# One level of Strassen for h on 11 pairs of row tiles, with a new order of the work

## The chip, the core and the metric

The kernel runs on one core of a Trainium2 chip. The metric is the device time of one execution in microseconds (us). TensorE (PE) does the matrix products, VectorE (DVE), ScalarE (ACT) and GpSimd (POOL) the elementwise work, and SyncE (SP) issues the DMAs. Each engine works through its own queue in order; semaphores join the queues.

## The reference, cut to what matters

A linear attention over 8 batches of 8 heads (576 positions, 64 wide) gives x of 4608 rows by 512. Then comes the layer that the change is about:

```python
h = x @ w_in                                  # 4608x512 by 512x1024
e = np.exp(h - h.max(-1)); sm = e / (e.sum(-1) + 1e-9)
solu = h * sm
ln = (solu - mean) / sqrt(var + 1e-6) * g_ln  # over each row's 1024
out = ln @ w_out                              # 1024x512
```

## The kernel before

The 4608 rows are 36 row tiles of 128 rows, named by batch and part and numbered 0 to 35 in the order in which they are made. Batches with an odd number have a fifth tile, which holds the last 64 rows of two batches.

The work is cut into generators, one for each key, and `ORDER` is a list, written out by a planner, of which generator takes its next step. The list is the program order: what it places on one engine runs there in that order. A suffix `.v` puts a step that has a choice on VectorE in place of ScalarE or GpSimd; `*3` means three steps. The keys are: `LK`, `LQ`, `V` loads; `K3` the keys of batch 3 up to the head matrices `bd`; `Q3a`, `Q3c`, `R3` the query softmaxes; `w0` to `w3` and `y0` to `y3` the two weight matrices, which come as 64-bit words and are put together on ScalarE and VectorE; `W` and `Z` their scaling and their split in two f16 halves (a high half and what is left, `wi[:, 0]` and `wi[:, 1]`, likewise `wo`); `P` idle matmuls that fill TensorE early on.

For each row tile t, `x` (L613 to L625) makes the transposed x in PSUM and copies it to SBUF as `xT`, again as a high and a low f16 half; two tiles share one such step. `h` (`hidden`, L640 to L704) makes h in a PSUM tile of two banks, of which there are two (`bufs=2`): 12 terms (high by high, low by high, high by low, over four chunks of 128 rows of w_in) times two halves of 512 columns, 24 matmuls of 128x512. The first four tiles are done in f32 instead (L640). The row's tail then works on h in PSUM: the maximum `top` on VectorE (L655), `nm` and the exponential `e` on ScalarE (L657, L661), a scale `ph` in tiny steps on GpSimd (L665 to L674), `h*ph*e` on VectorE (L677), `nmu`, the f16 high half `u` on ScalarE (L679, L682), the low half on VectorE (L684), the square on ScalarE (L691). A PSUM tile is free for the next h after that square. `u` is transposed by DMA into `uT` (L687), and `o` (`project`, L722) makes the output from `uT` and `wo` in 24 matmuls, later in the list.

Of the kernel before, what the change touches and what calls it, by code (L numbers as in the profile page):

```python
# [843 lines left out]
```

## Time and profile before

| | us |
|---|---|
| median of three runs | 457.14 (457.02 to 457.19) |
| profiled execution, first to last instruction (span) | 455.4 |
| around the span, median less span | 1.7 |
| busy: TensorE | 435.4 |
| busy: VectorE | 337.5 |
| busy: ScalarE | 276.0 |
| busy: GpSimd | 209.2 |

Times are of the one profiled execution; busy means that an instruction of the engine runs. A group's mean is the mean length of one instruction; since a next one can begin before the one in front has ended, the means add up to more than the busy time.

### The profile page before, as it was taken

The numbers are of one execution on the slowest core, as the hardware profiler recorded it, in microseconds if no ns is written. First come the engines' busy times: TensorE is split into PE (matmuls) and PEld (weight loads), VectorE is DVE, ScalarE is ACT, GpSimd is POOL, SyncE is SP. The second block draws the span as 40 slices with busy tenths as digits, with TensorE's granted clock in tenths as the row PEclk, the third lists the DMA queues.
The fourth block names the chain that finished last, engine by engine and source line by source line (L and its number), as shares of the span: only waits on it lengthen the run. The fifth ranks groups of instructions, "written<-read, shape, count | busy, mean of one in ns | idle before, by whom it ended". The sixth has DMA issues, their size and how long they took to land.

```text
span 455.4 us, 8734 instructions
## 1 busy us (share of the span) xinstructions
PE 435.4 (96%) x3351; PEld 208.4 (46%) x3351; DVE 337.5 (74%) x619; ACT 276.0 (61%) x477; POOL 209.2 (46%) x334
## 2 busy tenths in 40 slices
PE   0898899999999999999999999999999999999996
PEld 0543344454445445444544445444454444444445
DVE  5999999989788898769967869777967565443410
ACT  3889998685866656466657566556657444441331
POOL 4107885886774355734363375712423234211120
PEclk9999999999999999999999999999999999999999
DMA  8997699699779994996884787884436425334071
GB/s 276 394 317 276 124 199 173 166 224 185 176 155 211 199 244 63 221 212 148 180 210 91 158 190 167 191 201 97 107 64 136 94 46 117 69 79 84 24 186 46
DMA packets 167082, 73.98 MB, mean 162 GB/s; under 512 B 146424, under 2 KB 155904, under 8 KB 167040
## 3 DMA queue, kind: packets, MB, share of 16 engines
q1 hardware_dynamic: 167040, 73.42, 68.7%
q8 instruction: 26, 0.43, 0.4%
q14 instruction: 16, 0.13, 0.1%
HBM read 36.70 MB, written 9.44 MB: 101 GB/s over the span
## 4 chain that ended last, share of the span: by engine, by line
PE 87%; DVE 5%; DMA 3%; ACT 3%; issue 1%; POOL 1%; ACTq 0%; DVEq 0%; POOLq 0%
PE o L722 41%; PE h L648 37%; PE x L613 4%; PE kv L425 4%; DMA w_out<-in_moe_w_out_dram 2%; DMA qm<-in_q_dram 1%; PE h L640 1%; DVE qnmx L475 1%; DVE h L677 1%; DVE iw L269 1%; PE warm_up L779 1%; DVE iw L267 0%; POOL am L665 0%; ACT qm L479 0%; ACT e L691 0%
## 5 line engine op out<-in xcount | busy, mean ns | idle before, releaser
L722 PE MATMUL o<-wo,uT 128*128 128x512 f16 (+1 forms) x888 | 198.3, 373 | 0.0
L648 PE MATMUL h<-wi,xT 128*128 128x512 f16 x768 | 177.1, 379 | 0.0
L722 PEld LDWEIGHTS <-uT 128*128 128x128 f16 x888 | 85.7, 98 | 98.0 <-issue 1.8
L648 PEld LDWEIGHTS <-xT 128*128 128x128 f16 x768 | 74.3, 98 | 89.4 <-issue 1.0
L655 DVE TENSOR_REDUCE top<-h 128x1 f32<-128x1024 f32 x36 | 43.9, 1218 | 27.6 <-PE h L648 27.4
L684 DVE SCALAR_TENSOR_TENSOR u<-h,nmu,u 128x1024 f16<-128x1024 f32 x36 | 46.0, 1277 | 15.6 <-ACT u L682 15.2
L691 ACT ACTIVATE e<-h,nmu 128x1024 f32<-128x1024 f32 x36 | 40.0, 1112 | 25.4 <-DVE u L684 25.2
L677 DVE SCALAR_TENSOR_TENSOR h<-h,ph,e 128x1024 f32<-128x1024 f32 x36 | 46.3, 1285 | 7.9 <-POOL ph L674 4.6
L665 POOL TENSOR_SCALAR am<-nm 128x1 f32<-128x1 f32 x25 | 10.3, 412 | 88.6 <-ACT nm L657 88.6
L671 POOL TENSOR_TENSOR p<-pi,mone 128x1 f32<-128x1 f32 x36 | 24.2, 671 | 55.1 <-DVE pi L668 53.5
L682 ACT ACTIVATE u<-h,nmu 128x1024 f16<-128x1024 f32 x36 | 40.1, 1113 | 1.0
L732 ACT ACTIVATE os<-o,rr 128x512 f32<-128x512 f32 (+1 forms) x23 | 15.5, 674 | 31.9 <-PE o L722 16.6
L657 ACT ACTIVATE nm<-top,hs 128x1 f32<-128x1 f32 x28 | 8.2, 294 | 43.4 <-DVE top L655 43.4
L661 ACT ACTIVATE e<-h,nm,hs 128x1024 f32<-128x1024 f32 x28 | 33.7, 1203 | 0.7
L679 ACT ACTIVATE nmu<-s 128x1 f32<-128x1 f32 x36 | 7.3, 202 | 42.0 <-DVE h L677 39.8
L640 PE MATMUL h<-iw,xT 128*128 128x512 f32 x64 | 29.8, 601 | 2.4 <-ACT e L691 2.3
L502 POOL TENSOR_TENSOR qhl<-qm,qhl 128x512 f16<-128x512 f32 x24 | 28.1, 1191 | 7.2 <-ACT qhl L162 4.6
L495 POOL TENSOR_TENSOR qm<-qm,qrec 128x1024 f32<-128x1024 f32 x12 | 23.6, 1969 | 11.7 <-DVE qrec L486 10.7
L625 DVE SCALAR_TENSOR_TENSOR xT<-x,xT 128x512 f16<-128x512 f32 (+1 forms) x36 | 22.2, 622 | 8.5 <-ACT xT L623 8.5
L477 POOL TENSOR_TENSOR qm<-qm,qnmx 128x1024 f32<-128x1024 f32 (+1 forms) x12 | 23.5, 1964 | 8.4 <-DVE qnmx L475 8.4
L730 DVE TENSOR_SCALAR os<-o,rr 128x512 f32<-128x512 f32 (+1 forms) x14 | 10.2, 728 | 20.4 <-PE o L722 20.4
L623 ACT ACTIVATE xT<-x 128x512 f16<-128x512 f32 (+1 forms) x36 | 19.2, 542 | 8.5 <-PE x L613 8.5
(155 smaller groups left out, 539.4 us busy)
## 6 DMA issues: line engine op xcount, KB each, us to landing
km<-in_k_dram SPq DMA_DIRECT2D x7, 1152.0 KB, 7.5
vm<-in_v_dram SPq DMA_DIRECT2D x28, 288.0 KB, 4.5
out_dram<-os SPq DMA_DIRECT2D x31, 256.0 KB, 3.2
qm<-in_q_dram SPq DMA_DIRECT2D x7, 1024.0 KB, 6.4
wo<-in_moe_w_in_dram SPq DMA_DIRECT2D x4, 512.0 KB, 8.6
w_in<-in_moe_w_in_dram SPq DMA_DIRECT2D x4, 512.0 KB, 9.4
wo<-in_moe_w_out_dram SPq DMA_DIRECT2D x4, 512.0 KB, 5.6
w_out<-in_moe_w_out_dram SPq DMA_DIRECT2D x4, 512.0 KB, 8.9
```

What stands on the lines that cost most here:

```text
L495: on(nc.gpsimd).tensor_tensor(x, x, wide(rec), op=ALU.mult)
L502: on(nc.gpsimd).tensor_tensor(lo, y, hi, op=ALU.subtract)
L640: nc.tensor.matmul(h[:, ns], xT[:, kc], iw[kc][:, ns], start=(i == 0), stop=(i == NP - 1))
L648: nc.tensor.matmul(h[:, ns], xT[:, t, kc], wi[:, s, kc, ns], start=(i == 0), stop=(i == len(terms) - 1))
L655: nc.vector.tensor_reduce(top, h, axis=AX.X, op=ALU.max, negate=True)
L661: nc.scalar.activation(e, h, AF.Exp, bias=nm, scale=hs, accum_out=z)
L671: nc.gpsimd.tensor_tensor(p, pi, mone, op=ALU.pow)
L677: nc.vector.scalar_tensor_tensor(h, h, ph, e, op0=ALU.mult, op1=ALU.mult, accum_out=s1)
L682: nc.scalar.activation(u[:, 0], h, AF.Identity, bias=nmu)
L684: nc.vector.scalar_tensor_tensor(u[:, 1], h, nmu, u[:, 0], op0=ALU.add, op1=ALU.subtract)
L691: nc.scalar.activation(e, h, AF.Square, bias=nmu, accum_out=s2)
L722: nc.tensor.matmul(o, uT[:, j, f], wo[:, s, f, cols], start=(f == 0 and j == 0 and s == 0), stop=(f == NF - 1 and j == 1))
```

## The change

Eleven pairs of neighbouring row tiles (batches 2 to 7, parts 0/1 and 2/3, the last pair left out) get h by one level of Strassen's method in Winograd's form. x and w_in are cut in two by two blocks: two row tiles by two halves of the 512, and the two halves of the 512 by two halves of the 1024. Seven products (`product`, each 6 matmuls of 128x512) stand for the eight of before, 42 matmuls for 48. The sums of blocks of x are made once for a pair (`combined`, in place of the two copies in `attend`), those of w_in once for the kernel (`weights_combined`, key `T`). The seven products are summed on VectorE in both PSUM tiles of h (`hidden_twin`, keys `H9` to `H31`), which a pair takes at the same time; the sums that end a tile also give its row maximum, so that `hidden` of such a tile starts with `nm`. A pair's sums, splits and partial sums lie in three more SBUF tiles of the tag `uT`, whose buffers go from 12 to 13.

For every tile, the scale `ph` is made from the raw maximum `top` in place of `nm`, in three small steps for four, and the scales are carried in three columns (`[P, 3]`, which the cut diff leaves out).

`ORDER` is new as a whole; a small part is shown.

```diff
-BUFS = 12, 3, 2
+BUFS = 13, 3, 2
 FIRST = 3, 0, 2, 1
 WHOLE = 4
+TWINS = 2
 ON_VECTOR = 2
 ORDER = (
-    "LQ0 Q0b LK0 Q0b Q0a.v K0.v Q0b.v Q0a Q0b LQ0 K0 LK0 Q0c Q0b V00 K0.v Q0a K0.v V03.v K0.v V00 V03 V02 "
...
-    "W x3 K1 LQ1 h1.v*3 h2.v x3 y1 W h2 K1 h3 y3*2 K1.v K1 h2*2 V21 K1 h2 LK2 h2 Q1c y2 h2 h3 h1 K1 Z h1 "
-    "LQ1 h2.v h0 Z K1 Z K1 h1 h3 h1.v K1 Z K1 h2 h0 Z K1 Z*2 K1*2 Z V22 V23 Z*4 o1 Z h0 Z*2 h0 o0.v h3.v "
-    "x1 x4 Z S1 o0 h2.v o0 Z*4 o0.v x4 o0.v x4 h2*2 x4 h5.v V20 Q1c.v h3.v x4 Q0b.v Q1c.v h2.v o0 h3.v "
...
+    "LK0*2 K0*5 LQ0 K0 Q0b LQ0 Q0a Q0b*2 K0*2 V00 Q0b K0*2 V02 V00 Q0a*2 V03 K0 Q0b*2 Q0a Q0b V03 V01 Q0a "
...
+    "K1 P h1*3 Z*2 K2 W h2*2 K1 h0 h0.v W h0 K1 Z S1 Q1c h2 V21 K2 Z*2 K2*4 h2*2 K2 o0 Z*2 K1 W Z K1*2 Q1c "
+    "K1 Q1c h2 h3 K2 h3 h1.v h1 h3*2 Z K1 x4*2 h3 o0 h2*2 Z*2 LQ2 Z o0 R1 Z*4 h1 x4 V22 o0 Z*2 V23 Z*2 T h2 "
+    "T.v V20 x4 h3 h1 o1 h3*2 x6 h5 o0 h3 x4 W h3 h5 K2 T h3 T W h3*2 x6*2 h5*3 h3 o0 K2*2 h5 K2 h5*2 h5.v "
...
+    "x20 o14 h19 Q5c o14 h18 x20 h18 K5 x22*3 h18*2 h17 V62 K6.v h19*3 h16.v h19 x22*4 h15 o15 Q5c LQ6 h16 "
+    "o15*3 K6 x22 x20 h18*2 x24 h18 h19*2 x22 h19 R5*3 h18 o15 x22 Q6c h19 H20*2 Q6a H20*3 x24*5 K6*2 Q6c "
+    "H20*3 Q6c x24*3 o15 x22 x24 K6*2 Q6c*2 H20*3 K6*2 Q6c H20*3 h17.v h18*2 h20 h18 K6 h18 o18*2 h20*2 H20 "
+    "h20.v h21 h17.v h21 h21.v o18 h20 o18 h19.v o15 R5 h21*2 o18 K6 LK7 h20*2 h17 h21 o18.v Q6a o18 h21 x22 "
...
+    def weights_combined():
+        left, right = slice(0, DF // 2), slice(DF // 2, DF)
+        for j in range(2):
+            b11, b12, b21, b22 = (iw[kc][:, cols] for kc in (j, 2 + j) for cols in (left, right))
+            for out, x, y in ((b11, b12, b11), (b12, b22, b12), (b22, b22, b11), (b21, b22, b21)):
+                on(nc.gpsimd).tensor_tensor(out, x, y, op=ALU.subtract)
+                yield
+        s = iw["scale"]
+        for j in range(2):
+            t = wt[j] = sb.tile([P, 2, 2, DF], F16, name=f"wt{j}", tag="wd", bufs=WB)
+            for i in range(2):
+                x = iw[2 * i + j]
+                nc.scalar.activation(t[:, 0, i], x, AF.Copy, scale=s)
+                yield
+                nc.vector.scalar_tensor_tensor(t[:, 1, i], x, s, t[:, 0, i], op0=ALU.mult, op1=ALU.subtract)
+                yield
+    def right_block(name, s, i):
+        cols = slice(0, DF // 2) if name in ("11", "21", "t1", "t4") else slice(DF // 2, DF)
+        if name[0] == "t":
+            return wt[i][:, s, 0 if name in ("t1", "t3") else 1, cols]
+        return wi[:, s, 2 * (int(name[0]) - 1) + i, cols]
...
+        if row_tiles in twins:
+            yield from combined(name, row_tiles, accs)
+            return
...
+    def combined(name, row_tiles, accs):
+        t = sb.tile([P, 16 * P], F16, name=f"xT{name}", tag="xT", bufs=XB)
+        a11 = t[:, 0 : 4 * P].rearrange("p (s i k) -> p s i k", s=2, i=2)
+        side = t[:, 4 * P : 12 * P].rearrange("p (s i c k) -> p s i c k", s=2, i=2, c=2)
+        a21 = t[:, 12 * P : 16 * P].bitcast(F32).rearrange("p (i k) -> p i k", i=2)
+        x21, x11 = accs[0][:, :, 0], accs[0][:, :, 1]
+        x22, x12 = accs[1][:, :, 0], accs[1][:, :, 1]
+        sums = sb.tile([P, 4, 2, P], F32, name=f"sums{name}", tag="uT", bufs=UB)
+        split = sb.tile([P, 2, 4, 2, P], F16, name=f"split{name}", tag="uT", bufs=UB)
...
+        nc.scalar.activation(a21, x21, AF.Copy, scale=1.0 / QS)
+        yield
+        nc.scalar.activation(a11[:, 0], x11, AF.Copy, scale=1.0 / QS)
+        yield
+        nc.vector.scalar_tensor_tensor(sums[:, 2], x11, 1.0 / QS, a21, op0=ALU.mult, op1=ALU.subtract)
+        yield
+        nc.vector.scalar_tensor_tensor(a11[:, 1], x11, 1.0 / QS, a11[:, 0], op0=ALU.mult, op1=ALU.subtract)
+        yield
+        nc.scalar.activation(side[:, 0], accs[1], AF.Copy, scale=1.0 / QS)
+        yield
+        nc.vector.scalar_tensor_tensor(sums[:, 0], x22, 1.0 / QS, a21, op0=ALU.mult, op1=ALU.add)
+        yield
+        nc.vector.scalar_tensor_tensor(sums[:, 1], x11, -1.0 / QS, sums[:, 0], op0=ALU.mult, op1=ALU.add)
+        yield
+        nc.vector.scalar_tensor_tensor(sums[:, 3], x12, 1.0 / QS, sums[:, 1], op0=ALU.mult, op1=ALU.subtract)
+        yield
+        nc.vector.scalar_tensor_tensor(side[:, 1], accs[1], 1.0 / QS, side[:, 0], op0=ALU.mult, op1=ALU.subtract)
+        yield
+        cast(on(nc.scalar), split[:, 0], sums)
+        yield
+        on(nc.gpsimd).tensor_tensor(split[:, 1], sums, split[:, 0], op=ALU.subtract)
+        yield
+    def hidden_twin(row_tiles):
+        lefts = left_of[row_tiles[0]]
+        name = name_of(row_tiles[0])
+        def product(out, left, right):
+            terms = [(i, s, r) for i in range(2) for s, r in ((0, 0), (1, 0))] + [(i, 0, 1) for i in range(2)]
+            for n, (i, s, r) in enumerate(terms):
+                nc.tensor.matmul(
+                    out, lefts[left](s, i), right_block(right, r, i), start=(n == 0), stop=(n + 1 == len(terms))
+                )
+        vw = sb.tile([P, 2, DF // 2], F32, name=f"vw{name}", tag="uT", bufs=UB)
+        v_, w_ = vw[:, 0], vw[:, 1]
+        left, right = slice(0, DF // 2), slice(DF // 2, DF)
+        t1 = ps.tile([P, DF], F32, name=f"h{name_of(row_tiles[1])}", tag="h", bufs=2)
+        product(t1[:, left], "11", "11")
+        yield
+        t2 = ps.tile([P, DF], F32, name=f"h{name}", tag="h", bufs=2)
+        product(t2[:, left], "s2", "t2")
+        yield
+        cast(on(nc.scalar), w_, t1[:, left])
+        yield
+        product(t1[:, left], "12", "21")
+        yield
+        nc.vector.tensor_tensor(v_, t2[:, left], w_, op=ALU.add)
+        yield
+        product(t1[:, right], "s1", "t1")
+        yield
+        product(t2[:, right], "s3", "t3")
+        yield
+        product(t2[:, left], "22", "t4")
+        yield
+        tops = [sm.tile([P, 1], F32, name=f"top{name}_{i}", tag="ttop", bufs=8) for i in range(4)]
+        nc.vector.tensor_tensor_reduce(t1[:, left], t1[:, left], w_, 1.0, -3.0e38, ALU.add, ALU.max, tops[0])
+        yield
+        nc.vector.tensor_tensor(w_, t2[:, right], v_, op=ALU.add)
+        yield
+        nc.vector.tensor_tensor(v_, t1[:, right], v_, op=ALU.add)
+        yield
+        product(t1[:, right], "s4", "22")
+        yield
+        nc.vector.tensor_tensor_reduce(t2[:, left], w_, t2[:, left], 1.0, -3.0e38, ALU.subtract, ALU.max, tops[1])
+        yield
+        nc.vector.tensor_tensor_reduce(t2[:, right], t2[:, right], v_, 1.0, tops[1], ALU.add, ALU.max, tops[2])
+        done[row_tiles[0]] = t2, tops[2]
+        yield
+        nc.vector.tensor_tensor_reduce(t1[:, right], t1[:, right], v_, 1.0, tops[0], ALU.add, ALU.max, tops[3])
+        done[row_tiles[1]] = t1, tops[3]
+        yield
...
-            hs = hs_of[("rest", row_tile[0] // 2) if row_tile[1] == C else row_tile[0]]
-        top = sm.tile([P, 1], F32, name=f"top{name}", tag="htop")
-        nc.vector.tensor_reduce(top, h, axis=AX.X, op=ALU.max, negate=True)
+            scale = hs_of[("rest", row_tile[0] // 2) if row_tile[1] == C else row_tile[0]]
+        hs, low = scale[:, 0:1], scale[:, 1:2]
+        if row_tile not in done:
+            top = sm.tile([P, 1], F32, name=f"top{name}", tag="htop")
+            nc.vector.tensor_reduce(top, h, axis=AX.X, op=ALU.max, negate=True)
         nm = sm.tile([P, 1], F32, name=f"nm{name}", tag="nm")
-        nc.scalar.activation(nm, top, AF.Copy, scale=hs)
+        nc.scalar.activation(nm, top, AF.Copy, scale=scale[:, 2:3] if row_tile in done else hs)
         yield
         e = sb.tile([P, DF], F32, name=f"e{name}", tag="e", bufs=3)
         z = sm.tile([P, 1], F32, name=f"z{name}", tag="z")
@@ -662,16 +777,13 @@
         yield
         am = sm.tile([P, 1], F32, name=f"am{name}", tag="am")
-        on(nc.gpsimd).tensor_scalar(am, nm, -1.0, nm, op0=ALU.mult, op1=ALU.max)
+        on(nc.gpsimd).tensor_scalar(am, top, -1.0, top, op0=ALU.mult, op1=ALU.max)
         yield
         pi = sm.tile([P, 1], F32, name=f"pi{name}", tag="pi")
-        on(nc.gpsimd).tensor_scalar(pi, am, 0.5, 1.0 / US, op0=ALU.max, op1=ALU.mult)
-        yield
-        p = sm.tile([P, 1], F32, name=f"p{name}", tag="p")
-        nc.gpsimd.tensor_tensor(p, pi, mone, op=ALU.pow)
+        on(nc.gpsimd).tensor_scalar(pi, am, low, 1.0 / US, op0=ALU.max, op1=ALU.mult)
         yield
         ph = sm.tile([P, 1], F32, name=f"ph{name}", tag="ph")
-        on(nc.gpsimd).tensor_tensor(ph, p, hs, op=ALU.mult)
+        nc.gpsimd.tensor_tensor(ph, pi, mone, op=ALU.pow)
         yield
         s1 = sm.tile([P, 1], F32, name=f"s1{name}", tag="s1")
         nc.vector.scalar_tensor_tensor(h, h, ph, e, op0=ALU.mult, op1=ALU.mult, accum_out=s1)
...
+    twins = [[(b, c), (b, c + 1)] for b in range(TWINS, B) for c in (0, 2)][:-1]
...
+    works["T"] = weights_combined()
+    for group in twins:
+        works[f"H{tiles.index(group[0])}"] = hidden_twin(group)
```

## Rows read from the trace of the kernel before

**Rows 1.** The page: span, busy times, granted clock in 40 slices.

```profile
span 455.4 us, 8734 instructions
PE 435.4 (96%) x3351; PEld 208.4 (46%) x3351; DVE 337.5 (74%) x619; ACT 276.0 (61%) x477; POOL 209.2 (46%) x334
...
PEclk9999999999999999999999999999999999999999
```

**Rows 2.** Busy time of each engine in stretches of the span.

```profile
core 0: us, PE busy (x) PEld busy (x) DVE busy (x) ACT busy (x) POOL busy (x), PEclk, DMA share, GB/s
0.00:66.70 66.70, 50.06 (x473) 24.60 (x473) 59.49 (x111) 54.54 (x89) 34.26 (x40) 1.00 0.84 262
66.70:440.00 373.30, 373.30 (x2801) 176.21 (x2801) 277.54 (x508) 218.90 (x385) 174.92 (x295) 1.00 0.69 149
440.00:455.40 15.40, 12.01 (x80) 7.56 (x78) 0.48 (x1) 2.54 (x4) 0.00 (x0) 0.97 0.22 69
```

**Rows 3.** Line L613 from 60 to 70 us: length, start, what its engine waited for.

```profile
L613 PE MATMUL x<-qT,bd x16: 269/283/297, 66.7 to 67.5; 128*64 128x256 f16 x8, 64*64 64x256 f16 x8
...
  ACT wo L341: 0.8, 1
  DVE bd L458: 0.2, 1
```

**Rows 4.** The chain that ended last, 140 to 160 us: start, length, work.

```profile
149.37 5.18 PE h L648 x24
```

**Rows 5.** Groups on VectorE by shape: busy us, mean ns, idle before and its releaser.

```profile
L677 DVE SCALAR_TENSOR_TENSOR h<-h,ph,e 128x1024 f32<-128x1024 f32 x36 | 46.3, 1285 | 7.9 <-POOL ph L674 4.6 <-ACT e L661 2.7
L655 DVE TENSOR_REDUCE top<-h 128x1 f32<-128x1024 f32 x36 | 43.9, 1218 | 27.6 <-PE h L648 27.4
L625 DVE SCALAR_TENSOR_TENSOR xT<-x,xT 128x512 f16<-128x512 f32 x28 | 19.1, 682 | 5.5 <-ACT xT L623 5.5
L343 DVE SCALAR_TENSOR_TENSOR wo<-gw,gs,wo 128x512 f16<-128x512 f32 x8 | 5.5, 745 | 0.0
L677 DVE DVE_READ_ACCUMULATOR h<-h,ph,e 128x1 f32 x36 | 4.9, 137 | 0.0
L402 DVE TENSOR_TENSOR khalf<-khalf 128x512 f32<-128x512 f32 x7 | 4.9, 704 | 0.1
L625 DVE SCALAR_TENSOR_TENSOR xT<-x,xT 128x256 f16<-128x256 f32 x8 | 3.2, 410 | 3.0 <-ACT xT L623 3.0
```

**Rows 6.** The same on ScalarE and GpSimd.

```profile
L691 ACT ACTIVATE e<-h,nmu 128x1024 f32<-128x1024 f32 x36 | 40.0, 1112 | 25.4 <-DVE u L684 25.2
L502 POOL TENSOR_TENSOR qhl<-qm,qhl 128x512 f16<-128x512 f32 x24 | 28.1, 1191 | 7.2 <-ACT qhl L162 4.6 <-DVE qhl L164 2.2
L671 POOL TENSOR_TENSOR p<-pi,mone 128x1 f32<-128x1 f32 x36 | 24.2, 671 | 55.1 <-DVE pi L668 53.5
```

**Rows 7.** Instructions in order of time, the tail of the last row tile.

```profile
426.05 0.29 ACT L657 ACTIVATE nm<-top,hs 128x1 f32<-128x1 f32 x1 [2.16 <-DVE top L655]
...
427.25 1.20 ACT L661 ACTIVATE e<-h,nm,hs 128x1024 f32<-128x1024 f32 x1
428.34 0.20 ACT L661 ACTIVATION_READ_ACCUMULATOR e<-h,nm,hs 128x1 f32 x1
...
432.10 1.28 DVE L677 SCALAR_TENSOR_TENSOR h<-h,ph,e 128x1024 f32<-128x1024 f32 x1
...
433.47 0.20 ACT L679 ACTIVATE nmu<-s 128x1 f32<-128x1 f32 x1 [0.71 <-DVE h L677]
...
433.70 1.11 ACT L682 ACTIVATE u<-h,nmu 128x1024 f16<-128x1024 f32 x1
...
434.85 1.28 DVE L684 SCALAR_TENSOR_TENSOR u<-h,nmu,u 128x1024 f16<-128x1024 f32 x1 [1.42 <-ACT u L682]
436.17 1.11 ACT L691 ACTIVATE e<-h,nmu 128x1024 f32<-128x1024 f32 x1 [1.35 <-DVE u L684]
```

**Rows 8.** Busy time of each engine in the first 154 us (columns as in rows 2).

```profile
0.00:154.00 154.00, 137.37 (x1218) 66.46 (x1219) 135.91 (x252) 118.60 (x202) 92.16 (x120) 1.00 0.86 221
```

More of the change, by code (lines that the diff above doesn't have):

```diff
@@ L138, in linear_attention_solu_ffn @@
     nc.vector.memset(mone, -1.0)
-    one = cst.tile([P, 1], F32, name="one")
-    nc.vector.memset(one, 1.0)
-    isc = cst.tile([P, 1], F32, name="isc")
+    plain = cst.tile([P, 3], F32, name="plain")
+    for i, x in enumerate((1.0, 0.5, -1.0)):
+        nc.vector.memset(plain[:, i : i + 1], x)
+    isc = cst.tile([P, 3], F32, name="isc")
     vm = cst.tile([P, NP, KC, D + 1], F32, name="vm")
@@ L184, in pow2_scale @@
         nc.vector.tensor_scalar(p2.bitcast(I32), top.bitcast(I32), 0x7F800000, None, op0=ALU.bitwise_and)
-        inv = sm.tile([P, 1], F32, name=f"inv_{name}", tag="inv")
-        nc.vector.tensor_scalar(inv, p2, 2.0**-80, 2.0**-up, op0=ALU.max, op1=ALU.mult)
-        s = sm.tile([P, 1], F32, name=f"s_{name}", tag="s")
+        both = cst.tile([P, 3], F32, name="inv_in") if name == "in" else sm.tile([P, 3], F32, name=f"inv_{name}", tag="inv")
+        inv, s = both[:, 0:1], both[:, 1:2]
+        nc.vector.tensor_scalar(both[:, 0:3:2], p2.broadcast_to([P, 2]), 2.0**-49, 2.0**-up, op0=ALU.max, op1=ALU.mult)
         nc.vector.reciprocal(s, inv)
-        return s, inv
+        return s, both
     raw = {}
@@ L289, in weights_in_scaled @@
         yield from largest(m1, wide, "in")
-        s, inv = pow2_scale(tops["in"], 14, "in")
-        nc.vector.tensor_copy(isc, inv)
+        s, both = pow2_scale(tops["in"], 13, "in")
+        iw["scale"] = s
+        nc.vector.tensor_tensor(isc, both, plain, op=ALU.mult)
         yield
@@ L332, in weights_out_scaled @@
         yield from largest(m1, wide, "out")
-        s, inv = pow2_scale(tops["out"], 14, "out")
-        nc.vector.tensor_copy(osc, inv)
+        s, both = pow2_scale(tops["out"], 14, "out")
+        nc.vector.tensor_scalar(osc, both[:, 0:1], DF**0.5, None, op0=ALU.mult)
         gs = sm.tile([P, NF], F32, name="gs", tag="gs", bufs=1)
@@ L443, in keys @@
         yield from largest(mx, kv[:, 512 - P : 512], f"kv{b}")
-        s, inv = pow2_scale(tops[f"kv{b}"], 14, f"kv{b}")
+        s, both = pow2_scale(tops[f"kv{b}"], 11, f"kv{b}")
         t = bd[b % 3]
-        kv_of[b] = (t, inv)
+        kv_of[b] = (t, both)
         yield
@@ L569, in scales @@
     def scales(b):
-        hs = hs_of[b] = sm.tile([P, 1], F32, name=f"hs{b}", tag="hs")
+        hs = hs_of[b] = sm.tile([P, 3], F32, name=f"hs{b}", tag="hs")
         on(nc.gpsimd).tensor_tensor(hs, kv_of[b][1], isc, op=ALU.mult)
@@ L574, in scales @@
         if b % 2 == 1:
-            both = hs_of["rest", b // 2] = sm.tile([P, 1], F32, name=f"hsr{b}", tag="hsr", bufs=2)
+            both = hs_of["rest", b // 2] = sm.tile([P, 3], F32, name=f"hsr{b}", tag="hsr", bufs=2)
             nc.vector.tensor_copy(both[0:R], hs_of[b - 1][0:R])
@@ L626, in attend @@
             yield
-    def hidden(row_tile):
-        xT, name = xT_of[row_tile], name_of(row_tile)
-        h = ps.tile([P, DF], F32, name=f"h{name}", tag="h", bufs=2)
-        if row_tile in whole:
+    left_of, done = {}, {}
+    def combined(name, row_tiles, accs):
[7 more added lines that the diff above has]
+        split = sb.tile([P, 2, 4, 2, P], F16, name=f"split{name}", tag="uT", bufs=UB)
+        left_of[row_tiles[0]] = {
+            "11": lambda s, i: a11[:, s, i],
+            "12": lambda s, i: side[:, s, i, 1],
+            "22": lambda s, i: side[:, s, i, 0],
+            **{f"s{j + 1}": (lambda s, i, j=j: split[:, s, j, i]) for j in range(4)},
+        }
+        nc.scalar.activation(a21, x21, AF.Copy, scale=1.0 / QS)
[20 more added lines that the diff above has]
+        yield
@@ L637, in hidden @@
+    def hidden(row_tile):
+        name = name_of(row_tile)
+        if row_tile in done:
+            h, top = done[row_tile]
+        else:
+            xT = xT_of[row_tile]
+            h = ps.tile([P, DF], F32, name=f"h{name}", tag="h", bufs=2)
+        if row_tile in done:
+            scale = hs_of[row_tile[0]]
+        elif row_tile in whole:
             for i, kc in enumerate(FIRST):
@@ L641, in hidden @@
                 yield
-            hs = one
+            scale = plain
         else:
@@ L694, in hidden @@
         z1 = sm.tile([P, 1], F32, name=f"z1{name}", tag="z1")
[L695 removed]
+        on(nc.gpsimd).tensor_scalar(z1, z, 1e-9, ph, op0=ALU.add, op1=ALU.mult)
+        yield
         z2 = sm.tile([P, 1], F32, name=f"z2{name}", tag="z2")
+        on(nc.gpsimd).tensor_scalar(z2, z1, low, 2e-3 * DF**0.5, op0=ALU.mult, op1=ALU.mult)
         yield
[L698 removed]
         var = sm.tile([P, 1], F32, name=f"var{name}", tag="var")
[L700 to L701 removed]
+        on(nc.gpsimd).tensor_scalar(var, z2, z2, s2, op0=ALU.mult, op1=ALU.add)
         yield
```

5 lines of the change are left out of this document (1 added, 4 removed), and 112 rows, old and new, of the table ORDER.

## The prediction

> **What bounds the kernel now.** The page comes first: TensorE is busy for 435.4 of 455.4 us, and its granted clock is in the top tenth in every slice [rows 1]; no other engine passes 74%. Then the stretches, to see where the 20.0 us of TensorE's idle time lie [rows 2]. Up to 66.7 us it is busy for 50.06, so 16.6 us are lost there; from 66.7 to 440 us it is busy for 373.30 of 373.30; the last 15.4 us lose 3.4, while the last outputs are written. So there is a start that something else sets, a long middle that TensorE alone sets, and a short end.
>
> What sets the start is seen in the same rows: VectorE is busy for 59.49 of the first 66.7 us and idle for 7.2. The stretch was cut where TensorE last waits, at the first `x` of batch 1 (key `x4`), which begins at 66.7 us and whose named waits are a low half of `bd` on VectorE and a `wo` half on ScalarE [rows 3]. That gives a balance for any list. Add up the VectorE steps listed up to the one waited for, each at its group's mean less 0.055 us (by so much the means of all VectorE steps of the list, 372 us, exceed the 337.5 busy, for each of its instructions), add VectorE's idle time, and take away TensorE's work listed ahead of the waiting step: what is left is TensorE's idle time. The old list has 96 VectorE steps up to that half of `bd`, 59.9 us (measured 59.49), and 50.8 us of TensorE's work ahead of `x4`: 59.9 + 7.2 - 50.8 = 16.3, measured 16.6.
>
> **TensorE: 6 matmuls less for each pair.** Seven products of 6 stand for 48 matmuls of the same shape, so 11 x 6 = 66 go. A run of 24 took 5.18 us [rows 4], 0.216 each: 14.3 us less, in the middle stretch, where TensorE never waits. Everything else on TensorE stays, the seven idle-matmul steps `P` included. Its busy time becomes 421.1 us.
>
> **The other engines, all in all.** For each pair VectorE gets three additions of 512 columns (0.70 as the 512-column addition), four that also take a maximum (no such row; 0.75 to 0.89, from the 1024-column step that also sums, 1.285 and 0.137 for reading the sum, halved but for the fixed part; lower bound 0.61, half the maximum's 1.218; I take 0.84, since the instruction also writes PSUM and gives a sum out), five of 256 columns (0.41) and one of 512 (0.68): 8.2 us. It loses two maxima (1.218) and two low halves (0.682): 3.8 [rows 5]. That is +4.4, some +43 us over 11 pairs after the overlap of 0.055. The new list moves some 21 us of optional steps off VectorE (it does 3 of 16 key subtractions for 8, and none of the last steps of the query splits for 4), and `T` adds about 6: 365 us in all, some 81% of the span. ScalarE comes to about 306; GpSimd to about 255, since each pair's low split of 1024 columns costs twice 1.191 [rows 6]. None passes TensorE's 421 as a total, so the places decide. The Trainium skill speaks against the change here (Trainium Kernel Development and Optimization, section Best Practices: mind the pressure on PSUM, for what speeds up TensorE does not speed up emptying PSUM). By it the 14.3 us would turn into waits for VectorE, and the sum would be 457, no change. The trace agrees for the first 66.7 us only: from there on TensorE waits for nothing with VectorE busy for 277.5 of 373.3 us [rows 2].
>
> **The start: TensorE waits longer.** In the new list the keys come first, and the two steps that hand over `wo` are mixed with early steps of batch 2 and with `K1`. The same balance there: the worst place is the third step of `o0`, where the sixth chunk needs the sixth low half of `wo` (L343). Up to that half the list has 116 VectorE steps, 69.5 us: against the old 59.9, five more halves of `wo` and the steps ahead of them 3.5, seven opening steps of `K2` 3.3, queries 2.0, a fourth `h` tile's maximum and small steps 1.6, an `xT` copy 0.3, less a low half of `wi` 1.2. TensorE has 55.0 us ahead: 50.8, one `x` more (1.0) and 15 matmuls of `o0` (3.2). Lag 14.5 for 9.1, so +5.4 us, and TensorE's idle time there becomes 22.0. The first step of `x4` (lag 13.6) and the last of `h5` (13.0) stand close to it, so that no single one of these matters. The bounds: VectorE's idle time in that stretch is taken from before, 7.2, of which 5 pass until the first data land; it could be 5 to 10, so 20 to 25 us of idle TensorE. If the neighbouring steps run ahead of the list the loss is nothing.
>
> **The middle: a pair takes both h tiles.** Before, one h tile was filled while the other's tail ran. Now the next pair waits until both squares are done. What covers that is TensorE's work listed between the last product of a pair (`s4`) and the first of the next: 8.7 to 9.8 us in seven of the ten gaps (outputs of earlier tiles and one `x`, as between `H18` and `H20`), 16 to 19 in three. What must fit: the tail of one tile, by the last row tile where little else runs, is `nm` 0.29, `e` 1.20 and 0.2, then from 432.10 to 437.28 `h*ph*e`, `nmu`, `u`, low half, square, 5.2 us, in strict turns with 0.03 us between engines [rows 7]. Two tails share ScalarE, 4.1 us each. The first tile's two sums stand before or beside `s4`, so its `nm` can begin some 1.6 us before `s4` ends; the second's begins 0.85 after. Stepping through both queues with these durations, the first square ends 6.8 us after `s4` and the second 8.1. The list puts other steps between: on ScalarE 0 to 3.9 us a gap, 1 us in most. The first product of the next pair needs one of the tiles, and the second, 1.3 us later, the other. So most gaps just hold, and the one from 18 to 20 (3.9 us of others, 9.8 of cover) lacks some 0.9.
>
> Inside a pair, the third product overwrites what ScalarE copies out after the first (`w_`, 0.68 by a 512-column copy); in most pairs only the second product (1.30) lies between. Behind the copy in ScalarE's queue stand the copies of a later pair's x and the key exponentials; if a square (1.11) is still running when the first product ends, the copy ends at 1.8 and TensorE loses 0.5. The fourth product's neighbours give the two additions of `s4` time enough: 1.5 us against 3.6 to 6.5 of TensorE's work.
>
> Lower bound 0: the middle had no wait at all, with VectorE at 74%. Upper: 1 us a gap in seven gaps and 0.5 in eleven pairs, 12. I take 3, nearer the lower end, since the list leaves cover at each place.
>
> **At no cost.** The raw maximum lets `am` start a `nm` earlier and spares one GpSimd step; this ends VectorE's waits for `ph` (4.6 us in all [rows 5]), which TensorE's matmuls cover anyway; without that cover it would be a gain of at most 4.6. `T`'s last low half stands right ahead of `H9`, whose products read it: VectorE's work up to there is 116.4 us and TensorE's 105.9, a lag of 10.5, less than the start's 14.5, so TensorE's loss at the start covers it; late it would hold up `H9` alone. The wider scales are the same instructions. The last 23 us of TensorE's list are outputs with hardly a VectorE step among them, as before: 3.4 us of idle time at the end stay.
>
> **The sum**, against the profiled execution's own time: 435.4 - 14.3 = 421.1 busy; idle 22.0 at the start, 3 in the middle, 3.4 at the end: span 449.5. With 1.7 around the span, as before (455.4 against the median of 457.1), **451.2 us**.
>
> **Rivals.**
> (a) The start is no longer. For it: the lag is a list's, and TensorE may run ahead of it where nothing is needed. Against: by the same sum the old start came out within 0.3 us. Then 5.4 us and the middle's 3 come back: 443 us.
> (b) VectorE stays the bound beyond the start. Up to the low half of `bd` that `x13` needs, the new list has 141 us of VectorE's work (2.7 of it by the dearer pair steps), TensorE 132.4. With as much idle VectorE as before in the first 154 us, 154.0 - 135.9 = 18.1 [rows 8], TensorE has lost 26.8 by then, 4.8 more: 456 us. Against it: a fuller queue idles less. For it: VectorE is busy for 89% of those 154 us already.
> (c) On the other side: the two tails do not overlap but follow one another. The second tile's `nm` then waits for the first's square, 5.4 us after `s4`, and its own square ends 6.9 later, at 12.3, against 10.0 to 11.1 (the cover and the first product): 1.2 to 2.3 in each of seven gaps, some 12 us, 463 us. From an excess of 1.0 a gap on, 7 us, the kernel is slower than before. For it: the square waits for the low half though it reads nothing of it (25.2 us of ScalarE's idle time end so [rows 6]), so readers of one tile take turns. Against: the two tiles lie in different banks, and the list mixes the two tails.
>
> **Chances.** About 0.2%, 0.9 us, is what a measurement of this kernel tells from no change. The forecast with its bounds (446 to 455) 0.60; (a) 0.14; (b) 0.12, a third of it each way and a third within 0.9 us; (c), in part or whole, 0.14, of which 0.09 slower and the rest about even or just faster. Faster 0.80, same 0.07, slower 0.13. The range leaves out the best of (a) and the worse half of (c): 444 to 458.
>
> **What would show it.** Matmuls of h for the pairs: 462 for 528, each pair's time on TensorE shorter by 1.3 us without its waits. TensorE's idle time up to the first outputs about 22 us, the wait there named at `wo` or `bd`. From there to the end few waits; those that there are, at a pair's first two products for a square, or at its third for the copy. VectorE's busy time 355 to 375. The prediction is wrong if VectorE's idle time at the start differs by more than some 3 us from 7.2, or if the gaps between pairs show 1 us of waiting each.

## The result, and the profile after

The changed kernel takes 463.35 us (median of 4 runs, 462.33 to 463.79) against 457.15 before: a ratio of 1.0133, interval 1.0119 to 1.0147. It is 1.3% slower; 451.2 was forecast.

The page of the changed kernel, cut to the lines that answer to [rows 1]:

```profile
span 461.6 us, 8813 instructions
PE 426.9 (92%) x3285; PEld 203.4 (44%) x3285; DVE 373.9 (81%) x733; ACT 300.2 (65%) x532; POOL 258.8 (56%) x334
PE   0898777999999999989999999999999999999996
DVE  4899999999989999998988999988978875641600
PEclk9999989999999999999999999999999999999999
```

TensorE has the 66 matmuls less (3285 for 3351), but only 8.5 us less busy time. Now the stretches, cut as in [rows 2] where TensorE's last wait of the start ends (the wait for `wo` at L355, at 78.9 us):

```profile
0.00:78.90 78.90, 55.51 (x496) 26.77 (x497) 70.42 (x132) 58.97 (x101) 36.95 (x41) 0.98 0.84 242
78.90:430.00 351.10, 344.24 (x2641) 162.21 (x2641) 297.16 (x590) 233.16 (x419) 219.03 (x285) 1.00 0.68 149
430.00:461.60 31.60, 27.10 (x150) 14.38 (x147) 6.29 (x13) 8.09 (x15) 2.79 (x10) 1.00 0.33 83
```

| TensorE, us | forecast | measured |
|---|---|---|
| busy | 421.1 | 426.9 |
| idle at the start | 22.0 | 78.90 - 55.51 = 23.4 |
| idle in the middle | 3 | 351.10 - 344.24 = 6.9 |
| idle at the end | 3.4 | 31.60 - 27.10 = 4.5 |
| span | 449.5 | 461.6 |

Two of TensorE's groups by shape, the f32 matmuls of h and the largest group of the pairs:

```profile
L753 PE MATMUL h<-iw,xT 128*128 128x512 f32 x64 | 31.5, 634 | 2.7 <-ACT e L803 2.6
L693 PE MATMUL h<-wt,split 128*128 128x512 f16 x198 | 46.6, 379 | 0.9 <-DVE wt L301 0.9
```

The f32 group was 29.8 us long before: 1.7 us of the busy time are a stretch of 3.4 us at half clock (1.2 GHz), the 8 in PEclk. It lies at 65.4 to 68.8 us, begins 1.5 us after a wait of TensorE's of 1.9 us, and ends while TensorE runs f32 matmuls without a gap. The second row shows why the rest, some 4 us, is waiting too: one matmul is modelled as 379 ns long, while the next starts 216 ns after it, so the first 0.16 us of any wait count as busy time. To see such waits, the starts of the matmuls in the trace were taken apart by the steps of the list: the time from a step's first matmul to the next step's, less the number of its matmuls at the undisturbed pace (so a step is charged with the wait of the step behind it). Against that pace TensorE lost 12.1 us up to `x4` and `o0` before and 21.8 after, and from there to `h33` 2.8 and 14.0; matmuls saved, 14.2. Of the 14.0, output steps have 6.6 (1.3 before), x products 4.1 (nothing before), and the pairs' own products 1.5, of which 1.0 is one wait at H9.

What TensorE waited for after 96 us, by the view of waits (total, times, longest):

```profile
PE o L834 <- ACT os L844: 1.8, 5, 0.5
PE x L625 <- DVE xT L640: 1.1, 1, 1.1
PE kv L158 <- DVE mx L453: 1.1, 1, 1.1
PE h L693 <- DVE wt L301: 0.9, 1, 0.9
PE h L693 <- DVE vw L723: 0.6, 2, 0.3
PE h L693 <- ACT e L803: 0.4, 1, 0.4
```

Small waits at many places, all named on VectorE and ScalarE, and only 0.4 us in which a pair waits for a square.

### The profile page after: what moved, and what is told of

Same layout as the page of the kernel before. It is cut to its first block, busy times and chain, and to the rows that moved or that the text cites. A ratio compares the mean times of both kernels' runs of the same rounds, so it can differ in the third digit from the quotient of the medians.

```text
span 461.6 us, 8813 instructions
## 1 busy us (share of the span) xinstructions
PE 426.9 (92%) x3285; PEld 203.4 (44%) x3285; DVE 373.9 (81%) x733; ACT 300.2 (65%) x532; POOL 258.8 (56%) x334
## 4 chain that ended last, share of the span: by engine, by line
PE 45%; DVE 23%; POOL 9%; DMA 8%; ACT 6%; issue 6%; SPq 1%; DVEq 0%; POOLq 0%; ACTq 0%
PE o L834 23%; PE h L693 14%; PE h L761 6%; DMA qm<-in_q_dram 3%; DVE u L796 2%; DVE qsum L494 2%; DMA km<-in_k_dram 2%; PE kv L437 2%; DVE h L789 2%; DMA qT<-qhl 1%; DMA vm<-in_v_dram 1%; POOL qhl L514 1%; ACT e L776 1%; ACT e L803 1%; DVE top L770 1%
## 5 line engine op out<-in xcount | busy, mean ns | idle before, releaser
L834 PE MATMUL o<-wo,uT 128*128 128x512 f16 (+1 forms) x888 | 194.8, 373 | 3.2 <-ACT os L844 1.8
L761 PE MATMUL h<-wi,xT 128*128 128x512 f16 x240 | 54.2, 379 | 0.8 <-ACT e L803 0.7
L514 POOL TENSOR_TENSOR qhl<-qm,qhl 128x512 f16<-128x512 f32 x28 | 33.8, 1228 | 26.9 <-ACT qhl L146 23.7
L693 PE MATMUL h<-wt,split 128*128 128x512 f16 x198 | 46.6, 379 | 0.9 <-DVE wt L301 0.9
L816 POOL TENSOR_TENSOR r<-var,mhalf 128x1 f32<-128x1 f32 x36 | 22.5, 626 | 33.4 <-DVE var L813 32.7
L489 POOL TENSOR_TENSOR qm<-qm,qnmx 128x1024 f32<-128x1024 f32 (+1 forms) x15 | 27.7, 1855 | 21.3 <-DVE qnmx L487 21.1
L693 PEld LDWEIGHTS <-split 128*128 128x128 f16 x264 | 25.6, 98 | 31.8 <-issue 1.3
L423 POOL TENSOR_TENSOR km<-km,kb 128x1152 f32<-128x1152 f32 x13 | 35.3, 2722 | 3.0 <-issue 1.8
L761 PEld LDWEIGHTS <-xT 128*128 128x128 f16 x240 | 23.4, 98 | 29.1 <-issue 1.8
L507 POOL TENSOR_TENSOR qm<-qm,qrec 128x1024 f32<-128x1024 f32 x13 | 25.0, 1922 | 13.9 <-DVE qrec L498 10.7
L693 PE MATMUL h<-wi,xT 128*128 128x512 f16 x132 | 32.1, 379 | 0.4 <-ACT e L803 0.4
L844 ACT ACTIVATE os<-o,rr 128x512 f32<-128x512 f32 (+1 forms) x27 | 18.1, 676 | 18.9 <-PE o L834 12.2
L693 PEld LDWEIGHTS <-xT 128*128 128x128 f16 x198 | 19.2, 98 | 24.8 <-issue 2.3
L786 POOL TENSOR_TENSOR ph<-pi,mone 128x1 f32<-128x1 f32 x36 | 22.5, 625 | 6.5 <-DVE pi L783 4.1
```

What stands on the lines that cost most here:

```text
L423: on(nc.gpsimd).tensor_tensor(km[:, ns], km[:, ns], wide, op=ALU.subtract)
L489: on(nc.gpsimd).tensor_tensor(x, x, wide(nmx), op=ALU.add)
L514: on(nc.gpsimd).tensor_tensor(lo, y, hi, op=ALU.subtract)
L693: nc.tensor.matmul(out, lefts[left](s, i), right_block(right, r, i), start=(n == 0), stop=(n + 1 == len(terms)))
L761: nc.tensor.matmul(h[:, ns], xT[:, t, kc], wi[:, s, kc, ns], start=(i == 0), stop=(i == len(terms) - 1))
L834: nc.tensor.matmul(o, uT[:, j, f], wo[:, s, f, cols], start=(f == 0 and j == 0 and s == 0), stop=(f == NF - 1 and j == 1))
```

## The experiments

**One part at a time.** First the old list with no pairs and with the new tail and scales; then the new list with the pairs' tiles as plain tiles.

```diff
- twins = [[(b, c), (b, c + 1)] for b in range(TWINS, B) for c in (0, 2)][:-1]
+ twins = [[(b, c), (b, c + 1)] for b in range(TWINS, B) for c in (0, 2)][:0]
```

> The changed kernel without any pair and with the old list (the step that the new tail no longer has is taken out of it): only the raw-maximum row scale, the three-column scales and the thirteenth uT buffer are new. Theory V (VectorE's work ahead of TensorE is the bound, far beyond the start, and neither the tail nor the scales matter): TensorE has its old 435.4 us of work behind the old start, 457 us, within 1. Rival T (the shorter tail or the wider scales change the time by themselves): it differs from 457 by 2 us or more.

Measured: 458.47 us, 1.0029 (1.0018 to 1.0040) of before. Not quite even: one three-column copy on VectorE takes 2.27 us (the view of the tile `hsr`, minimum, median and maximum in ns), and `h9` loses 1.2 us behind it.

```profile
L602 DVE COPY hsr<-hs x4: 141/154/2273, 121.1 to 387.9; 64x3 f32<-64x3 f32 x4
```

> The new list with the pairs' tiles computed as before, each from 24 matmuls: the first twelve steps of a pair's products become the six steps of either tile, and the weights' differences are not formed. Theory V: the new list's start still costs 23 to 24 us of TensorE's idle time for 16.6 and a stretch at half clock, and from batch 2 on there is no wait, since the pairs' VectorE work is gone: 435.4 + 1.7 + 23.5 + 4.5 + 1.7 = 467 us, range 463 to 468. Rival L (the new list is no worse by itself, and all of the loss comes with the pairs' products): 457 to 459 us.

Measured: 475.84 us, 18.7 more than before, above the ranges of both theories. Up to `o0` it loses 21.6 us against the pace, as much as the changed kernel (21.8): the new list's start is dearer without any pair. It loses another 11 after `o0`, 3.8 of them behind squares where plain tiles stand in the pairs' places. So this list is not one for plain tiles, and the 12.5 us between it and the changed kernel bound the pairs' own worth only roughly.

**VectorE made lighter, early and late.**

```diff
- nc.vector.tensor_reduce(shaped(sums), x, axis=AX.X, op=ALU.add)
+ few = slice(0, D // 4) if relieved else slice(0, D)
+ nc.vector.tensor_reduce(shaped(sums), x[..., few], axis=AX.X, op=ALU.add)
```

> The changed kernel, but from batch 2 on VectorE takes the maximum and the sum of the query softmax of the main rows over 16 of each 64 values; the other 48 are left out of both. That takes some 12 x 2 x 0.87 = 21 us off VectorE from about 110 us on and changes nothing of the pairs, of PSUM, of ScalarE or of GpSimd. Theory V: the waits from 100 us on (some 10 to 12 us, half of them too short to be shown as idle) go, the start stays: 453 to 456 us. Rival C (the pairs wait for one another through the two h tiles, whatever VectorE does) and rival S (ScalarE's queue holds them up): 462 to 463.5 us.

> The changed kernel, but for batches 0 and 1 alone VectorE takes the maximum and the sum of the query softmax over 16 of each 64 values: 7.2 us less for VectorE, all of it ahead of the first outputs. Theory V: VectorE is the bound from there to about 360 us, so what it saves at the start comes off the end: 456 to 459 us, with TensorE's idle time of the first 100 us 4 to 7 us shorter and the later waits as they were. Rival M (the middle has slack, and a start that ends earlier only meets the same waits later): 461 to 463.5 us, with more waiting after 100 us.

Measured: 460.33 and 462.01 us, 3.0 and 1.3 less than the changed kernel; the second is hardly told from it (its interval, 1.0068 to 1.0122 of before, overlaps 1.0119 to 1.0147). Theory V falls short in both: VectorE is not the one bound. The first time lies in neither theory's range, the second in rival M's, and its trace bears M out: the waits named after 96 us add up to 7.4 us for 5.9. In both traces one more of VectorE's scale copies of the rest tiles is long (1.92 and 1.93 us for 0.17), and with one softmax subtraction they are 2 to 3 us longer together than in the changed kernel, which eats part of the relief and points to the copies.

**The old start before the new list.** The old list up to the first step of `o0`, then all of the new one that is not yet done.

> The changed kernel, but its list begins with the old list up to the first step of o0; from there on the new list goes on with all that is not yet done. Up to x4 and o0 TensorE lost 21.8 us against the pace of its matmuls in the changed kernel and 12.1 before. Theory S (the new list's start is a loss of its own, 9.7 us): that comes back, 452 to 456 us. Theory N (VectorE, ScalarE and GpSimd are all nearly full up to 125 us, so the old start only moves the wait behind it, to x9 and H9): 458 to 463 us, with 5 us or more lost between o0 and H9.

Measured: 468.59 us. Theory N's kind of result, and above its range: `o0` waits at once.

```profile
PE o L835 <- DVE wo L356: 12.6, 1, 12.6
```

The opening steps of `K2` and steps of `Q1c`, which the new list has done by then, stand ahead of the last steps of `wo` in this list. The start is lost in one place or the other.

**GpSimd, the scale copies, and the old list with pairs.**

```diff
- on(nc.gpsimd).tensor_tensor(out, x, y, op=ALU.subtract)
+ on(nc.gpsimd).tensor_tensor(out[:, 0:64], x[:, 0:64], y[:, 0:64], op=ALU.subtract)
```

> The changed kernel, but GpSimd forms the weights' differences for 64 of 512 columns; the other 448 are left as they were. That takes some 8 us off GpSimd between 92 and 107 us. Theory G (GpSimd, on the chain without a break from 91 to 124 us, is the bound there, behind VectorE's): the waits at x9, at the first products of H9 and at o5 (2.8 us) go, 460 to 462 us. Theory V (VectorE alone): 463 us.

Measured: 461.96 us, ratio 1.0110 (1.0090 to 1.0130). The interval overlaps the changed kernel's; the trace has 10.2 us at half clock for 3.4, so a gain may be hidden in it. The waits at `x9` and at H9's first products are gone, the one at `o5` is not. Undecided.

```diff
- nc.vector.tensor_copy(both[R:P], hs[R:P])
+ nc.scalar.copy(both[R:P], hs[R:P])
```

> The changed kernel, but ScalarE makes the eight copies of the scales of the rest tiles for VectorE. Theory W (the three-column copy on VectorE is held until a GpSimd instruction ends, 1.22 and 1.82 us for 0.1 to 0.17, and the wait of 1.3 us at x18 comes from the second of these): both long copies go, the wait at x18 goes, 461 to 462.3 us. Rival: x18 waits for something else, and nothing changes.

Measured: 459.24 us, 4.1 less, more than was expected. In the changed kernel, in order of time around the longest copy (VectorE, GpSimd and TensorE alone):

```profile
203.30 2.13 POOL L682 TENSOR_TENSOR split<-sums,split 128x1024 f16<-128x1024 f32 x1
...
203.63 1.82 DVE L590 COPY hsr<-hs 64x3 f32<-64x3 f32 x1
...
205.48 1.28 DVE L796 SCALAR_TENSOR_TENSOR u<-h,nmu,u 128x1024 f16<-128x1024 f32 x1
205.60 0.41 PE L625 MATMUL x<-qT,bd 128*64 128x256 f16 x4
206.69 0.41 DVE L640 SCALAR_TENSOR_TENSOR xT<-x,xT 128x256 f16<-128x256 f32 x1
...
207.15 0.75 PE L625 MATMUL x<-qT,bd 128*64 128x256 f16 x12 [1.14 <-DVE xT L640]
```

A copy of 192 numbers takes 1.82 us and ends when GpSimd's subtraction ends (205.43). Behind it in VectorE's queue stand a low half of `u` and the low half of `xT` for which the x product then waits.

> The old list with the pairs put in by a rule: the steps of a pair's products stand evenly where its two tiles' matmuls stood, both tails where that of the later tile stood, the differences between h3 and H9, and the single tiles behind a pair that frees their PSUM. The pairs' instructions are the same as in the changed kernel. Theory S (the pairs save their 14.2 us wherever a list leaves them room, and the new list's order is what is lost): the old start, 12.1 us lost, and a middle that loses 3 to 12: 446 to 456 us. Theory V (VectorE's added work has to be waited for in any list): 457 us or more.

Measured: 617.59 us. Theory S misses, and V's "457 us or more" holds by its number alone: what the pairs wait for here is mostly a square on ScalarE.

```profile
PE h L708 <- ACT e L818: 47.6, 10, 11.6
PE h L776 <- ACT e L818: 19.0, 5, 7.5
PE h L708 <- DVE vw L738: 12.9, 9, 3.3
```

Ten waits of 4.8 us for a square, though this list too has work between the pairs, 24 to 60 output matmuls (5 to 13 us) and more. The squares come late: the first ends 12 to 21 us after a pair's last product `s4`, the second 1 us behind it. What holds them up was not taken apart. The rows shown are 80 of TensorE's 144 idle us, and its granted clock was 0.90 in this run. In the new list the first squares end 8.1 to 10.6 us after `s4` in the seven short gaps, the next pair begins 8.8 to 11.4 after it, and the wait for squares is 0.4 us in all.

**The scales, one column at a time.**

```diff
- nc.vector.tensor_copy(both[R:P], hs[R:P])
+ for j in range(3):
+     nc.vector.tensor_copy(both[R:P, j : j + 1], hs[R:P, j : j + 1])
```

> The changed kernel, but VectorE copies the scales of the rest tiles one column at a time, three instructions for one, as the old kernel's single column was copied. Theory W (it is the three-column form that a GpSimd instruction holds up; a one-column copy is never held): no copy of these takes more than 0.2 us, and the time is that of the kernel whose copies ScalarE makes, 459.2, within 1 us. Rival: any copy on VectorE at these places is held, the long ones stay, and the time is 463.

Measured: 460.95 us, 2.4 less than the changed kernel. The copies behave as theory W has it; the time is 1.7 above the other kernel's, outside the 1 us allowed, and its trace has a second stretch of 3.4 us at half clock. At the place shown above:

```profile
201.58 2.12 POOL L683 TENSOR_TENSOR split<-sums,split 128x1024 f16<-128x1024 f32 x1
201.91 0.28 DVE L591 COPY hsr<-hs 64x1 f32<-64x1 f32 x3
```

Three copies in 0.28 us, beside the same subtraction.

```diff
- nc.vector.tensor_scalar(both[:, 0:3:2], p2.broadcast_to([P, 2]), 2.0**-49, 2.0**-up, op0=ALU.max, op1=ALU.mult)
+ for j in (0, 2):
+     nc.vector.tensor_scalar(both[:, j : j + 1], p2, 2.0**-49, 2.0**-up, op0=ALU.max, op1=ALU.mult)
```

> The kernel with the scales of the rest tiles copied by ScalarE (459.2 us), and the two columns of the inverse scale written by two one-column instructions. Theory W: the inverse for the scale of the keys, held for 0.3 to 0.6 us in two batches, is not held any more, and as it stands ahead of the block matrix that the x products wait for, 0 to 1 us comes back: 458.2 to 459.2. Rival: the additional instruction costs 0.1 us a batch and nothing comes back.

Measured: 456.41 us (454.99 to 458.35), 0.9987 of before (0.9974 to 1.0000). With both mendings the change is 6.9 us faster than as it was made, and about even with the kernel before. The inverses are not held any more, as theory W has it, but 2.8 us come back where 0 to 1 was expected. VectorE's groups, the first three of the changed kernel, the last two of this one:

```profile
L470 DVE SCALAR_TENSOR_TENSOR bd<-kvn,inv_kv,bd 64x256 f16<-64x256 f32 x16 | 10.9, 681 | 0.2
L590 DVE COPY hsr<-hs 64x3 f32<-64x3 f32 x4 | 3.4, 844 | 0.1
L171 DVE TENSOR_SCALAR inv_kv<-p_kv 128x2 f32<-128x2 f32 x8 | 2.2, 272 | 0.3
```

```profile
L470 DVE SCALAR_TENSOR_TENSOR bd<-kvn,inv_kv,bd 64x256 f16<-64x256 f32 x16 | 8.4, 525 | 0.2
L171 DVE TENSOR_SCALAR inv_kv<-p_kv 128x1 f32<-128x1 f32 x16 | 1.7, 149 | 0.3
```

The inverses held in the changed kernel (0.53 us for w_in, 0.50 and 0.66 for the keys, each 0.17 otherwise) make 1.2 us. More of VectorE's time, 2.5 us, comes from the low half of `bd`, which this edit does not touch. In the changed kernel, and with the copies alone, it comes behind the held inverse for w_in and runs beside GpSimd's subtraction of the keys; here it begins 0.43 us before that (first the changed kernel, then this one):

```profile
38.10 0.53 DVE L171 TENSOR_SCALAR inv_in<-p_in 128x2 f32<-128x2 f32 x1
...
39.99 2.95 DVE L470 SCALAR_TENSOR_TENSOR bd<-kvn,inv_kv,bd 64x256 f16<-64x256 f32 x1
40.02 5.40 POOL L423 TENSOR_TENSOR km<-km,kb 128x1152 f32<-128x1152 f32 x2
```

```profile
39.23 0.48 DVE L470 SCALAR_TENSOR_TENSOR bd<-kvn,inv_kv,bd 64x256 f16<-64x256 f32 x1
...
39.66 5.23 POOL L423 TENSOR_TENSOR km<-km,kb 128x1152 f32<-128x1152 f32 x2
```

So part of the gain is what happens to fall beside what in this list. How the 2.8 us divide is not shown; the profiled execution is the slowest of the twelve.

**Loads, and VectorE once more.** Batch 1's four loads of values listed together (`V10 V12 V11 V13`), and the light queries in all batches, both with the copies on ScalarE.

> The kernel with the scales of the rest tiles copied by ScalarE (459.2 us), with the four loads of batch 1's values issued together, ahead of nine other loads and transpositions in SyncE's queue. TensorE's two waits for them at K1 (1.3 us by the trace, just ahead of the stretch at half clock) go. Theory V (VectorE's queue sets the start, and TensorE's waits ahead of x4 only change their names): less than 0.5 us comes back, unless the half clock goes too, which gives 1.7. Rival D (the transfers set the start): 1.3 us or more without a change of the clock.

Measured: 460.92 us, 1.7 worse than without the move. The waits for the values go, and one at the f32 matmuls of h, for a square, grows from 2.2 to 4.7 us. Theory D falls; V's "no gain" holds, not its reason.

> The kernel with the scales of the rest tiles copied by ScalarE (459.2 us), and in all batches VectorE takes the maximum and the sum of the main rows' query softmax over 16 of each 64 values; the others are left out: 28 us less on VectorE. The two halves of this alone gave 3.0 and 1.4 us. Theory N (VectorE, ScalarE, GpSimd and the transfers are laid out as tightly as one another, so that relief of one soon meets the next): 455 to 457 us, TensorE still losing 16 us or more up to o0. Theory V: 449 to 453 us.

Measured: 454.93 us; VectorE's busy time falls by 22.6 us (370.3 to 347.7), the time by 4.3, and up to `o0` 19.9 us are still lost. Theory N.

**The clock.** Steps of four idle matmuls (`P`) ahead of waiting steps of the start, then fewer of those that are in the list.

```diff
- ... W K0 W y3 x2 x2.v P y2*3 x2 h0 y0 LQ1 K0 h0*3 V12 x3*2 ...
+ ... W K0 W y3 x2 x2.v P y2*3 x2 h0 y0 LQ1 K0 h0*3 V12 P x3*2 ...
```

> The kernel with the mended scales (copies on ScalarE, inverse by column; 456.4 us, whose profile has 10.2 us at half clock up to 52 us of its span), and nine more steps of four idle matmuls in the start, each ahead of a step of TensorE that waits. Theory K (the half clock is part of the start's loss): the clock stays at full speed up to the outputs, and 1.5 to 3.5 us come back, 453 to 455 us. Rival V (TensorE's slower work is hidden behind VectorE's): the clock stays up and the time is 456 to 458, as the idle matmuls take some time of their own.

> The changed kernel as it is, with the same nine steps of idle matmuls. Theory K: its one stretch of 3.4 us at half clock goes, 1 to 1.7 us come back, 461.5 to 462.5 us. Rival V: 463 to 464.5 us.

> As the kernel with the mended scales and nine steps of idle matmuls, but with sixteen. If nine were too few to hold the clock, it stays up here, and the time is 453 to 455 us; if nine were enough, the seven more cost up to 0.9 us each where TensorE does not wait as long, 454 to 458 us.

Measured: 460.19, 465.01 and 464.16 us, all worse, and above the ranges of all theories. The lists of the first two have eight more steps and not nine (60 idle matmuls in the traces for 28). They leave one stretch of 3.4 us at half clock in both traces; sixteen more leave none before the last output, and cost 7.8 us all the same. (The half clock named for the mended kernel lies up to 70 us of its span, not 52.)

> The kernel with the mended scales (456.4 us) without the last three of its seven steps of idle matmuls, 2.6 us of TensorE's time. Theory P (TensorE's work at the start is on the path for about half of its time, as the added steps showed): 454.5 to 456 us, if the clock does not fall further. Rival K (without them TensorE stays longer at half clock): 457 to 460 us, with more than 10.2 us of half clock in the trace.

> The kernel with the mended scales without any idle matmuls, 6.1 us of TensorE's time less. Theory P: 453 to 455 us, if the clock does not fall further. Rival K: the clock falls for longer, and the time is 457 us or more.

Measured: 457.05 (454.85 to 458.30) and 457.58 us (456.25 to 459.76). The first is not told from 456.41; the second is 1.2 us worse (1.0001 to 1.0020 of before, against 0.9974 to 1.0000). Theory P falls for the steps that are there. Rival K's time comes in the second, but not its reason: both traces have 3.4 us at half clock, for 10.2 with the steps. So the half clock, 1.7 us in the changed kernel's f32 matmuls, is not what makes the start long, and idle matmuls don't give it back.

**The scales in the old list.**

> The old list with the new tail and no pairs, its scales mended (copies on ScalarE, inverse by column). Theory W: the 2.27 us of one copy, behind which h9 waited for 1.2 us, are gone, and the time is that of the kernel before, 457.0 to 457.5 us. Rival: the shorter tail or the row scale cost something of their own, and it stays at 458.5.

Measured: 457.18 us, 1.0001 of before (0.9993 to 1.0010). As theory W has it: new tail and row scale cost nothing, the wider scales as written cost 1.3 us even there.

## Why the prediction was wrong

**The step that failed** is "The wider scales are the same instructions", costed at nothing. They are the same operations in another form, and the form can be held up by GpSimd. Mended, the changed kernel gains 6.9 us (463.35 to 456.41: 4.1 by the copies, 2.8 by the inverses and what falls in place behind them) and the old list 1.3 (458.47 to 457.18). No rival named it. Without it the change is even with the kernel before; with it, 1.3% slower. It is 6.9 of the 12.2 us by which the forecast missed. The other 5.2 belong to a second step: the terms for the start and the middle were too small, the middle most.

**The matmuls**: right. 66 are gone, 14.2 us at the pace.

**The start**: right in kind and place, short in size. VectorE's work up to the sixth low half of `wo` was put at 69.5 us and is 70.42; its idle time at 7.2 and is 8.5; the last wait is there. Idle TensorE is 23.4 us for 22.0, inside the bounds. But by the pace this start costs 9.7 us more than the old one (21.8 for 12.1), where 5.4 was forecast: waits and half clock that count as busy are not in the balance. Missing were 1.7 us of half clock, and the low half of `bd` at 40 us, which takes 2.95 us beside a subtraction of the keys on GpSimd. Rival (a) falls, and e2 shows that this start needs no pair to be slow.

**The middle**: mis-sized, and in the wrong places. Instead of 3 us there are 6.9 of idle time and 4 more that count as busy, 11.2 by the pace, within the bound of 12. The gaps between pairs and the copy of `w_`, for which the 3 was reckoned, hardly wait at all. The waits are at x products, outputs and H9's weights, and part of them comes from the held scales: with the copies on ScalarE the loss from `o0` to `h33` falls from 14.0 to 10.9 us against the pace.

**VectorE as the bound, rival (b)**: partly. It was forecast at 365 us and takes 373.9. The additions cost 0.69 for 0.70, the ones with a maximum 0.68 to 0.76 and 0.13 to 0.14 for reading it out, 0.82 to 0.90 in all for 0.84. But 22.6 us off VectorE give 4.3 us (e12): it is one of several queues with little slack. The Trainium skill's rule of PSUM pressure (Trainium Kernel Development and Optimization, Best Practices), which the page states for TensorE tiling, gave 457 in the prediction. The mended kernel's 456.4 agrees with that size alone: waits for PSUM are not its cause here (0.4 us for squares).

**Rival (c)**: its 463 us is what was measured, by chance, for the two tails do overlap. One of the short gaps (the last product of a pair, `s4`, is the first line, the next pair's first product the last; TensorE's work between them and other steps are left out):

```profile
348.56 1.46 PE L693 MATMUL h<-wi,split 128*128 128x512 f16 x6
...
349.46 0.29 ACT L772 ACTIVATE nm<-top,hs 128x1 f32<-128x1 f32 x1 [3.91 <-DVE top L729]
...
350.99 0.28 ACT L772 ACTIVATE nm<-top,hs 128x1 f32<-128x1 f32 x1
...
356.80 1.11 ACT L803 ACTIVATE e<-h,nmu 128x1024 f32<-128x1024 f32 x1
...
358.04 1.11 ACT L803 ACTIVATE e<-h,nmu 128x1024 f32<-128x1024 f32 x1
358.64 1.46 PE L693 MATMUL h<-wi,xT 128*128 128x512 f16 x6
```

The second `nm` begins 5.8 us before the first square, and the squares end 1.2 us apart; in e8 they end 1.0 to 1.2 apart as well. Their times were reckoned too early (6.8 and 8.1 us after `s4`; here 8.1 and 9.3, up to 10.6 and 12.6 in other short gaps), so the cover held with little to spare.

**What stays open**: the mended kernel is still 5.2 us above the forecast, and why is not shown. Its trace (of an execution of 458.35 us, with 10.2 us at half clock) loses 21.3 us against the pace up to `o0` and 10.7 from there to `h33`, for 12.1 and 2.8 before. No single engine, load or clock stretch tried here accounts for that; a list planned anew for the mended scales was not tried.

## What to carry to other kernels

A change of an operand's shape is an edit with a price: look up what form the instruction takes and what runs beside it, even when it handles a few hundred numbers. Where several in-order queues are full, a microsecond taken from one gave back a fifth of it (4.3 us of 22.6), while 2.7 us of held copies cost 2.4 to 4.1 (e9 and e7). And before blaming the large part of a change, run its small parts alone in the old order: here that run (e1) is the one whose trace shows one long copy and the wait behind it.
